# Block-sparse attention with an MLP: the second batch from dense to gathered attention, masks and transposes on TensorE, and a new order of work

## The chip, the cores and the metric

The kernel runs on one core of one Trainium2 chip. A core has five engines, each with its own in-order stream of instructions: TensorE (PE, with its weight loads as PEld), VectorE (DVE), ScalarE (ACT), GpSimd (POOL) and SyncE (SP, which here only issues transfers). They meet through semaphores. The metric is the device time of one execution in microseconds; less is better.

## The reference

Four batches of attention with eight heads, 768 tokens and 64 numbers per head, followed by an MLP over all 3072 tokens (512 to 2048 to 512). Attention is sparse in blocks of 32 tokens, 24 blocks to a side:

```python
scores = (q @ k.T) / sqrt(64)
blk_i, blk_j = pos[:, None] // 32, pos[None, :] // 32
mask = abs(blk_i - blk_j) <= 1
mask = mask | (blk_i == 0) | (blk_j == 0) | (blk_i == 23) | (blk_j == 23)
for qb in range(24):
    for kb in sampled_blocks[qb]:          # three drawn key blocks per query block
        mask[qb*32:(qb+1)*32, kb*32:(kb+1)*32] = True
attn = softmax(where(mask, scores, -1e9))
x = concat over heads of (attn @ v)        # 3072 x 512
out = relu(x @ w_in)**2 @ w_out            # float32
```

The first and the last block of queries see all keys; every other block sees its neighbours, the first and last key block and the three drawn ones.

## The kernel before, in words

A unit `u` is one batch and one pair of heads: 16 units, `HP` = 4 per batch. Matrix work is done in bf16 with 64-row halves of TensorE in pairs (helper `pair`, the line L203 of nearly all matmuls in the profile).

Batches below `SB` (here 2) are **dense**. For a unit, 256 queries and two chunks of 128 keys, `scores` (L343) puts 128 x (2 heads x 2 chunks x 256 queries) into one of four PSUM tiles `X`, ScalarE takes the exponential (`exps`, L360), VectorE multiplies by the 0/1 mask (`masks`, L367) and `values` adds up the product with V, a column of ones giving the sum (`normalize`, L410 and L413). For the first 256 queries of batch 0 the mask is instead added to the scores on TensorE, as a product of two small matrices `oh` and `R2` (argument `add`). The mask tiles for `masks` are kept in the buffers called VG, and are built by `mask_tile` and `mask_evac` from the ranges in `MASKED`.

Batches from `SB` on are **gathered**: for 128 queries, a visit (six per batch), only the keys and values of wanted blocks are brought together. `v_store` writes a batch's V to DRAM; `v_gather` fetches drawn rows with indirect transfers from GpSimd, or with SP's by block numbers in registers; `v_window` fetches the neighbours; `k_gather` (L593 to L599) copies the wanted columns of K into `KG`, on GpSimd or VectorE, with block numbers that `load_blocks` has put in registers (L561). Then `s_scores`, `s_exps` (L623), `s_masks` (L630), `s_values` (L653), `s_normalize` (L659, L662), and `s_transp` turns the 128 x 512 result by a DMA transpose on SP into `xT`.

Queries and keys of batch 0 are transposed on TensorE (`transp`, L305, with `evac`), those of units 4 to 15 by DMA (`transp_dma`). Results of batch 0 are transposed on TensorE (`x_transp`), of batch 1 by DMA (`x_transp_dma`).

The MLP runs in tiles of 256 tokens: `hidden` (product with `w_in`), `relu` (L707 ScalarE, L709 VectorE), `square` (L718 ScalarE, L720 GpSimd), `output` (product with `w_out`), `out_copy` from PSUM to `ys`, and `store`. The last tile's output is split into pieces. Weights come in eight parts, issued by GpSimd (`w_load`, four of w_in and four of w_out); `loads_gate` holds SP's loads for units 4 and on until parts 6 and 7 have come.

The order of everything is one long table, `PROGRAM`: each word has the engine's letter (P, V, A, G, S), the number of a task, and for those that take a PSUM tile its place. `run_program` issues the tasks in this order, so that each engine does its own tasks in the order of its letters, and waits where a task's input isn't ready. The program is written for this one fixed set of buffers.

Of the kernel before, what the change touches and what calls it, by code (L numbers as in the profile page):

```python
# [25 lines left out]
def kernel(  # L26
# [34 lines left out]
    SB, VR, KG_BUFS, VG_BUFS = 2, D + 2, 2, 3  # L61
# [404 lines left out]

    def table_places(e):
# [5 lines left out]
        for i in range(P // block):  # L473
            G.iota(lane[i * block:(i + 1) * block], pattern=[[0, 1]], base=0, channel_multiplier=1, **small)

    def table_slots(e):
        tmp = RT[tb["tmp"][0].at]
        n = SL - 4
        tri, eq = (tmp[0:GR, i * n * SL:(i + 1) * n * SL].rearrange("g (s z) -> g s z", z=SL) for i in range(2))
        al, sm = (tmp[0:GR, 2 * n * SL + i * 2 * SL:2 * n * SL + (i + 1) * 2 * SL].rearrange("g (a s) -> g a s", a=2) for i in range(2))  # L480
        same = tmp[0:GR, 256:256 + 2 * SL * n_rand].rearrange("g (a s r) -> g a s r", a=2, r=n_rand)
        low[0] = RT[tb["tmp"][1].at][0:D].bitcast(BF)[:, 0:5 * P].rearrange("g (s c) -> g s c", c=P)
        V.tensor_copy(out=tab.rearrange("o (g s) -> o g s", s=TS)[:, :, 0:RS],
                      in_=sb_r[:, 2 * n_rand:2 * n_rand * (nb - 1)].rearrange("o (g s two) -> o g s two", g=GR, two=2)[:, :, :, 0])
        V.memset(low[0], 0.0)
        V.tensor_copy(out=ids[:, 6:SL], in_=sb_g.rearrange("g (s two) -> g s two", two=2)[:, :, 0])
        V.tensor_tensor(out=eq, in0=ids[:, 4:SL, None].broadcast_to([GR, n, SL]), in1=ids[:, None, :].broadcast_to([GR, n, SL]), op=AOP.is_equal)
        V.scalar_tensor_tensor(out=eq, in0=before, scalar=0.0, in1=eq, op0=AOP.is_gt, op1=AOP.mult)
        V.tensor_reduce(out=dup, in_=eq, axis=AX.X, op=AOP.max)
        V.tensor_tensor(out=al, in0=ids[:, None, :].broadcast_to([GR, 2, SL]), in1=bl[:, :, None].broadcast_to([GR, 2, SL]), op=AOP.subtract)  # L490
        V.tensor_scalar(out=sm, in0=al, scalar1=-1.0, scalar2=None, op0=AOP.is_ge)
        V.scalar_tensor_tensor(out=al, in0=al, scalar=1.0, in1=sm, op0=AOP.is_le, op1=AOP.mult)
        V.tensor_tensor(out=same, in0=ids[:, None, :, None].broadcast_to([GR, 2, SL, n_rand]),
# [5 lines left out]
        V.tensor_scalar(out=dup, in0=dup, scalar1=-1.0, scalar2=1.0, op0=AOP.mult, op1=AOP.add)  # L499
        V.tensor_tensor(out=al[:, :, 4:SL], in0=al[:, :, 4:SL], in1=dup[:, None, :].broadcast_to([GR, 2, n]), op=AOP.mult)  # L500
        def spread(j, of):
# [8 lines left out]
        V.tensor_scalar(out=half, in0=lane, scalar1=float(HB), scalar2=-float(HB), op0=AOP.is_ge, op1=AOP.mult)  # L510
        V.tensor_tensor(out=lane, in0=lane, in1=half, op=AOP.add)
# [11 lines left out]
    def table_rows(e):  # L523
        V.tensor_scalar(out=idx, in0=low[1][:, P:P + GR], scalar1=float(HB), scalar2=lane, op0=AOP.mult, op1=AOP.add)
        load_blocks("POOL")
        load_blocks("DVE")
        load_blocks("SP")

    def table_masks(g0, g1, e):
        n = g1 - g0  # L530
        for c in range(3):
            copy(e, MKS[:, g0:g1, c].rearrange("p g (e a i) -> p (g e) a i", e=2, a=2) if 0 else MKS[:, g0:g1, c].rearrange("p g (e a i) -> p g e a i", e=2, a=2),
# [36 lines left out]
    def load_blocks(e):  # L569
        for g in wanted[e]:  # L570
# [94 lines left out]
    def s_transp(b, v, e):  # L665
        sy.dma_start(out=x_tile(b, v // 2 * QW)[:, :, v % 2 * P:v % 2 * P + P], in_=xtile.pop(("s", b, v)).rearrange("p a h d -> p (a h d)"), transpose=True)
# [129 lines left out]
    def prepare(u):  # L796
# [4 lines left out]
        if u >= HP:  # L801
# [5 lines left out]
            for w in (1, 0):  # L807
# [4 lines left out]
                x = T_(transp_dma, u, w, deps=[c] + old_s, put=[qc])  # L812
# [131 lines left out]
    for us in [range(b * HP, (b + 1) * HP) for b in range(B)]:  # L944
        for u in us:
            prepare(u)
# [142 lines left out]
```

## Time and profile before

| | us |
|---|---|
| three runs | 261.31, 259.39, 261.24 (median 261.24) |
| profiled execution | 258.88 |
| its span | 257.1 |
| busy: TensorE / ScalarE / VectorE / GpSimd | 243.1 / 183.6 / 171.3 / 98.8 |
| exponentials, dense (72) / gathered, large (48) | 70.6 / 38.0 |
| mask multiplications, dense (60) | 40.9 |
| squares on GpSimd, 1024 wide (11) | 21.6 |

The profile is of one execution; the span is the part of it between the first and the last instruction, and 1.8 us of the execution lie outside. Busy times say how long an engine had an instruction in it. On TensorE, whose instructions overlap in a pipeline, the ends of matmuls are modelled, so its busy time is more than its work at full rate. The line numbers are those of the kernel above; most copies have line L121 or L123 (helper `copy`), and are told apart by their tiles.

### The profile page before, as it was taken

Reading aid. Unit: us, or ns where it says so; the run is one execution under the profiler, and the core shown is the slowest. Engines: PE = TensorE matmul, PEld = TensorE weight load, DVE = VectorE, ACT = ScalarE, POOL = GpSimd, SP = SyncE. Lnnn points to the kernel's source line nnn. Section 1 sums busy time; section 2 is a strip of 40 time slices with the busy share of each in tenths; the row PEclk is TensorE's granted clock in tenths of the full one; section 3 lists DMA queues with packets and bytes.
Section 4 is the critical chain, followed back from the end, with each engine's and each line's share of the span. In section 5 each row is a group of like instructions: output and inputs, shape, how many; then the busy total and the mean of one; then the engine's idle time right before and its main releaser. Section 6 shows DMA issues by size and latency. Waiting matters only on the chain.

```text
span 257.1 us, 12061 instructions
## 1 busy us (share of the span) xinstructions
PE 243.1 (95%) x5265; PEld 182.1 (71%) x5265; DVE 171.3 (67%) x408; ACT 183.6 (71%) x217; POOL 98.8 (38%) x178
## 2 busy tenths in 40 slices
PE   7888999999999997998998999999999999999993
PEld 4667879678874677975864867866875677767683
DVE  7778988899889995969916756657536725730301
ACT  3899999998999797846783975675965286623640
POOL 3183247003316026198556314264357620412100
PEclk9999999999999999999999999999999999999999
DMA  6999989999999996999699779998474923044022
GB/s 200 374 250 207 206 205 155 270 202 252 250 281 179 197 202 153 340 229 154 188 243 202 194 174 167 251 214 199 129 206 95 189 40 60 5 121 148 23 86 83
DMA packets 64692, 47.08 MB, mean 183 GB/s; under 512 B 31567, under 2 KB 60624, under 8 KB 64640
## 3 DMA queue, kind: packets, MB, share of 16 engines
q1 hardware_dynamic: 58512, 37.82, 64.7%
q0 software_dynamic: 5440, 8.05, 16.8%
q8 instruction: 41, 0.67, 1.1%
q10 hardware_dynamic: 688, 0.46, 0.6%
q14 instruction: 11, 0.09, 0.1%
HBM read 35.51 MB, written 7.91 MB: 169 GB/s over the span
## 4 chain that ended last, share of the span: by engine, by line
PE 53%; DVE 5%; DVEq 1%; issue 1%; ACT 1%; ACTq 0%
PE X L203 49%; PE X L653 4%; DVE VB L123 1%; ACT pT L623 1%; DVEq L561 1%; DVE MKS L123 1%; DVE pT L630 1%; DVE r L709 0%; DVE KG L599 0%; DVE qc L123 0%; DVE XS L413 0%; DVE KG L593 0%; DVE XS L662 0%; DVEq L599 0%; DVE rs L410 0%
## 5 line engine op out<-in xcount | busy, mean ns | idle before, releaser
L203 PE MATMUL X<-xT,w_in_sb 64*128 64x256 bf16 x1536 | 100.8, 269 | 2.8 <-issue 1.5
L203 PE MATMUL X<-w_out_sb,g 64*128 64x512 bf16 (+3 forms) x960 | 95.2, 334 | 0.1
L203 PEld LDWEIGHTS <-w_in_sb 64*128 64x128 bf16 x1536 | 74.6, 94 | 16.0 <-issue 5.4
L360 ACT ACTIVATE pT<-X 128x1024 bf16<-128x1024 f32 x72 | 70.6, 1030 | 7.6 <-PE X L203 6.8
L623 ACT ACTIVATE pT<-X 128x768 bf16<-128x768 f32 (+1 forms) x56 | 41.6, 766 | 26.5 <-PE X L203 23.9
L203 PEld LDWEIGHTS <-g 64*128 64x128 bf16 x960 | 40.3, 94 | 26.3 <-PE X L203 0.4
L720 POOL TENSOR_TENSOR g<-r 128x1024 bf16<-128x1024 f32 (+1 forms) x20 | 31.6, 1587 | 64.4 <-ACT r L707 47.2
L707 ACT ACTIVATE r<-X 128x1024 f32<-128x1024 f32 x28 | 29.8, 1068 | 20.6 <-PE X L203 20.5
L709 DVE TENSOR_SCALAR r<-X 128x1024 f32<-128x1024 f32 x20 | 24.5, 1224 | 26.7 <-PE X L203 13.7
L367 DVE TENSOR_TENSOR pT<-pT,VG 128x1024 bf16<-128x1024 bf16 x60 | 40.9, 715 | 0.2
L718 ACT ACTIVATE g<-r 128x1024 bf16<-128x1024 f32 (+1 forms) x40 | 35.2, 899 | 2.7 <-DVE r L709 2.5
L203 PE MATMUL X<-QKT 64*128 64x256 bf16 (+1 forms) x384 | 31.6, 250 | 3.3 <-DVE XS L413 1.3
L630 DVE TENSOR_TENSOR pT<-pT,MKS 128x768 bf16<-128x768 bf16 (+1 forms) x48 | 27.6, 607 | 10.7 <-ACT pT L623 10.5
L203 PEld LDWEIGHTS <-QKT 64*128 64x128 bf16 x384 | 16.7, 95 | 9.5 <-issue 4.1
L579 POOL DMA_INDIRECT VG<-rows,idx x19 | 20.2, 1061 | 4.4 <-issue 2.6
L203 PEld LDWEIGHTS <-pT 64*128 64x128 bf16 x768 | 16.0, 94 | 1.9
L203 PE MATMUL X<-VB,pT 64*128 64x65 bf16 x768 | 17.1, 190 | 0.0
L203 PEld LDWEIGHTS <-KG 64*128 64x128 bf16 x528 | 13.8, 95 | 4.5 <-issue 0.2
L659 DVE RECIPROCAL ss<-X 128x8 f32<-128x8 f32 x12 | 2.5, 206 | 19.5 <-PE X L653 17.3
L653 PEld LDWEIGHTS <-pT 128*64 128x64 bf16 x624 | 11.9, 111 | 4.9 <-issue 3.7
L203 PE MATMUL X<-QKT,KG 64*128 64x64 bf16 x528 | 15.3, 190 | 0.1
L123 POOL CAST VB<-vs 128x768 bf16<-128x768 f32 x9 | 7.8, 869 | 16.5 <-DMA vs<-in_v_dram 16.4
(107 smaller groups left out, 210.3 us busy)
## 6 DMA issues: line engine op xcount, KB each, us to landing
vs<-in_v_dram SPq DMA_DIRECT2D x14, 384.0 KB
ks<-in_k_dram SPq DMA_DIRECT2D x13, 384.0 KB
qs<-in_q_dram SPq DMA_DIRECT2D x12, 384.0 KB
out_dram<-ys SPq DMA_DIRECT2D x9, 512.0 KB
VG<-rows SPq DMA_DIRECT2D x20, 132.0 KB
w_in_sb<-in_moe_w_in_dram POOLq DMA_DIRECT2D x4, 512.0 KB, 8.6
w_out_sb<-in_moe_w_out_dram POOLq DMA_DIRECT2D x4, 512.0 KB, 9.9
rows<-VB SPq DMA_DIRECT2D x2, 792.0 KB
```

Of the source, the lines that this page charges most:

```text
L123: (V if e == "DVE" else G).tensor_copy(out=out, in_=in_)
L203: last = nc.tensor.matmul(out(r ^ crossed), lhsT(r ^ crossed, rows), rhs(r ^ crossed, rows), skip_group_check=True, **kw)
L360: A.activation(out=pT[:, :, 0:n], in_=stile.pop(a)[:, :, 0:n], func=AF.Exp, scale=scale)
L367: V.tensor_tensor(out=pT, in0=pT, in1=m[:, None].broadcast_to([P, 2, len(cs), w]), op=AOP.mult)
L579: G.indirect_dma_start(out=to[0:RS * HB], out_offset=None, in_=pairs, in_offset=bass.IndirectOffsetOnAxis(ap=idx[0:RS * HB, g - 1:g], axis=0))
L623: A.activation(out=pT[:, :, 0:n], in_=stile.pop((u, v, gs))[:, :, 0:n], func=AF.Exp, scale=scale)
L630: V.tensor_tensor(out=pT, in0=pT, in1=m[:, None].broadcast_to([P, 2, n]), op=AOP.mult)
L653: nc.tensor.matmul(po[i * D:(i + 1) * D, h, a * VW:(a + 1) * VW], pts[g][:, h, c * D:(c + 1) * D], val, start=a == 0 and c == 0, stop=c == ...
L707: A.activation(out=to, in_=src, func=AF.Relu)
L709: V.tensor_scalar(out=to, in0=src, scalar1=0.0, scalar2=None, op0=AOP.max)
L718: A.activation(out=g, in_=r, func=AF.Square)
L720: (G if e == "POOL" else V).tensor_mul(out=g, in0=r, in1=r)
```

## The change

`SB` becomes 1: batch 1, too, is done by gathering, so there are 18 visits instead of 12, and the table of drawn blocks is needed earlier. `MASKED` becomes empty: all masks of batch 0 are added on TensorE, and mask tiles and mask multiplications no longer exist. `BY_PE` names units 4 to 7, whose queries and keys are transposed on TensorE instead of by DMA. `s_transp` becomes eight TensorE transposes into spare columns of the visit's own PSUM tile, followed by a copy out (`s_evac`) on VectorE or ScalarE, which then frees the tile. The table's work is cut into five smaller tasks that use `ys` buffers instead of `r` buffers, and `load_blocks` into two parts per engine. The order of all tasks is new. A word with letter S for a transpose still means that the instruction is issued on TensorE at that place.

```diff
-    SB, VR, KG_BUFS, VG_BUFS = 2, D + 2, 2, 3
+    SB, VR, KG_BUFS, VG_BUFS = 1, D + 2, 2, 3
...
     GATES = (6, 7)
+    BY_PE = range(HP, 2 * HP)
-    MASKED = ((256, 512), (512, 768), (0, 256))
+    MASKED = ()
...
+    def table_scratch():
+        tmp = [YS[b_.at] for b_ in tb["tmp"]]
...
-    def table_slots(e):
-        tmp = RT[tb["tmp"][0].at]
...
+        low[0] = table_scratch()[-1]
+        G.memset(low[0], 0.0)
+
+    def table_ids(e):
...
+    def table_dup(e):
...
+    def table_near(e):
...
+    def table_drawn(e):
...
+    def table_low(e):
...
     def table_rows(e):
         V.tensor_scalar(out=idx, in0=low[1][:, P:P + GR], scalar1=float(HB), scalar2=lane, op0=AOP.mult, op1=AOP.add)
-        load_blocks("POOL")
-        load_blocks("DVE")
-        load_blocks("SP")
...
-    def load_blocks(e):
-        for g in wanted[e]:
+    def load_blocks(g0, g1, e):
+        for g in [g_ for g_ in wanted[e] if g0 <= g_ < g1]:
             if g not in held_at[e]:
                 held_at[e][g] = blocks_of(g, ENGINE[e])
...
-    def s_transp(b, v, e):
-        sy.dma_start(out=x_tile(b, v // 2 * QW)[:, :, v % 2 * P:v % 2 * P + P], in_=xtile.pop(("s", b, v)).rearrange("p a h d -> p (a h d)"), transpose=True)
+    def s_transp(b, v, buf, e):
+        xs = xtile.pop(("s", b, v))
+        pt = tile_of(buf)[:, :, 384:512].bitcast(BF).rearrange("p r (a i) -> p r a i", i=D)
+        for a in range(HP):
+            for r, rows in enumerate(HALVES):
+                nc.tensor.transpose(pt[:, r, a], xs[rows, a].rearrange("p h d -> p (h d)"), identb[rows, rows])
+        xtile["t", b, v] = pt
+
+    def s_evac(b, v, e):
+        to = x_tile(b, v // 2 * QW)[:, :, v % 2 * P:v % 2 * P + P]
+        copy(e, to.rearrange("q a (r i) -> q r a i", r=2), xtile.pop(("t", b, v)))
...
-                x = T_(transp_dma, u, w, deps=[c] + old_s, put=[qc])
+                if u in BY_PE:
+                    hb = Buf("X")
+                    t = T_(transp, u, w, ALL, hb, deps=[c], get=[hb], put=[qc])
+                    x = T_(evac, u, w, ALL, deps=[t] + old_s, put=[hb])
+                else:
+                    x = T_(transp_dma, u, w, deps=[c] + old_s, put=[qc])
...
-        nm = T_(s_normalize, b, v, deps=[va], get=[xs], put=[yb, ot])
-        mu["s", b, v] = T_(s_transp, b, v, deps=[nm] + x_get(b, v // 2 * QW), put=[xs])
+        nm = T_(s_normalize, b, v, deps=[va], get=[xs])
+        xt = T_(s_transp, b, v, yb, deps=[nm], put=[xs])
+        mu["s", b, v] = T_(s_evac, b, v, deps=[xt] + x_get(b, v // 2 * QW), put=[yb, ot])
...
-    tmp = tb["tmp"] = [Buf("r"), Buf("r")]
-    tb["slots"] = T_(table_slots, deps=[t, p], get=tmp)
+    tmp = tb["tmp"] = [Buf("ys"), Buf("ys")]
+    p = T_(table_places, get=tmp)
+    i_ = tb["ids"] = T_(table_ids, deps=[t, p])
+    for e_ in ("POOL", "DVE", "SP"):
+        T_(load_blocks, 0, 4, deps=[i_])
+        T_(load_blocks, 4, nb, deps=[i_])
...
-            attend(a, us[0] < HP and a[1] == 0)
+            attend(a, True)
...
-        A29 G35 P4/3 V32 P30/0 P12/2 P14/3 P9/1 P5/1 V31 P33/1 V111 P36/3 P0/2 A37 V1 V34 P102/2 V209 V46 P47/0 P106/1 A103 V48 P104/3
...
+        A36 P4/0 P37/1 P12/2 P14/3 G42 P9/0 P5/2 V39 V38 P40/3 P43/0 P0/2 V100 A44 V1 V41 P91/1 V53 V183 A92 P54/2 P95/0 V55 P93/3 V50
...
```

Three places of the new order follow. The first is GpSimd's stream at the start. Before, behind the copy that waits for the third load of V, stand the weight loads (`w_in_sb`, `w_out_sb`; a row with x2 is two parts), casts of V (`VB`) and of queries (`qc`), and squares (`g` from `r`):

```order
L328 DMA w_in_sb<-in_moe_w_in_dram 128x4x512 x2
L123 CAST VB_189<-vs_80 128x2x6x64
L123 CAST qc_107<-qs_74 128x512
L328 DMA w_in_sb<-in_moe_w_in_dram 128x4x512
L123 CAST VB_189<-ys_85 128x2x6x64
L123 CAST qc_109<-qs_75 128x512
L328 DMA w_in_sb<-in_moe_w_in_dram 128x4x512
L331 DMA w_out_sb<-in_moe_w_out_dram 128x4x512 x2
L720 TENSOR_TENSOR g_94<-r_81 128x512
L331 DMA w_out_sb<-in_moe_w_out_dram 128x4x512
```

Now the table's places (`MKS`, `ids`, `bl`, `lane`, `ys`) and one cast are ahead of two parts of w_out and the last of w_in:

```order
L485 MEMSET ys_86 64x640
L124 CAST qc_107<-KG_119 128x512
L332 DMA w_out_sb<-in_moe_w_out_dram 128x4x512 x2
L575 TENSOR_LOAD tab
L329 DMA w_in_sb<-in_moe_w_in_dram 128x4x512
L743 TENSOR_TENSOR g_95<-r_82 128x512 x2
```

and the other two parts of w_out come a dozen instructions later:

```order
L124 CAST qc_107<-ks_79 128x384 x2
L743 TENSOR_TENSOR g_98<-r_82 128x1024
L124 CAST VB_192<-vs_80 128x2x6x64
L332 DMA w_out_sb<-in_moe_w_out_dram 128x4x512 x2
L743 TENSOR_TENSOR g_99<-r_83 128x512 x2
```

So two parts of w_out (6 and 7, those that the gate waits for) moved ahead of the last part of w_in, and the other two behind squares and a cast of the second batch's V.

The second place is TensorE at the end of a visit. Before, as here behind the last visit in its order, a visit's value matmuls (`VG`, `pT`) were followed by hidden work:

```order
L653 MATMUL X_149<-VG_209,pT_90 64x65
L203 LDWEIGHTS w_in_sb
L203 MATMUL X_147<-xT_117,w_in_sb 128x256
L203 LDWEIGHTS w_in_sb
L203 MATMUL X_147<-xT_117,w_in_sb 128x256
```

Now, at the third visit of batch 3 for one, the transposes of the normalized result (`XS`) stand directly behind the last value matmul, eight pairs of rows of which the first and the last are shown here:

```order
L667 LDWEIGHTS pT_87
L667 MATMUL X_149<-VG_210,pT_87 64x65
L684 LDWEIGHTS XS
L684 MATMUL X_149<-identb,XS 128x64
...
L684 LDWEIGHTS XS
L684 MATMUL X_149<-identb,XS 128x64
L204 LDWEIGHTS KG_119
L204 MATMUL X_148<-QKT,KG_119 128x64
```

What moved is a step that was on SP's queue; it now stands in TensorE's stream between that visit's values and the scores of the next.

The third place is the end of SP's stream: stores of the output (`ys` and `qs` hold pieces of it). Before:

```order
L779 DMA out_dram<-ys_85 64x512
L781 DMA out_dram<-ys_85 128x512
L776 DMA out_dram<-ys_84 128x2x512
L776 DMA out_dram<-ys_85 128x512
L776 DMA out_dram<-qs_74 128x256
L776 DMA out_dram<-qs_76 128x128
```

Now:

```order
L802 DMA out_dram<-ys_86 64x512
L804 DMA out_dram<-ys_86 128x512
L799 DMA out_dram<-qs_77 128x128
L799 DMA out_dram<-ys_85 128x2x512
L799 DMA out_dram<-ys_86 128x512
L799 DMA out_dram<-qs_75 128x256
```

The store of the smallest piece, `qs` 128x128, moved from last to fourth from last; the three larger ones are behind it.

More of the change, by code (lines that the diff above doesn't have):

```diff
@@ L509, in table_slots @@
         spread(4, ids)
-        V.tensor_scalar(out=half, in0=lane, scalar1=float(HB), scalar2=-float(HB), op0=AOP.is_ge, op1=AOP.mult)
-        V.tensor_tensor(out=lane, in0=lane, in1=half, op=AOP.add)
     def table_spread(buf, e):
@@ L891, in visit @@
         cl = T_(v_claim, b, v, get=[vb], deps=mk_claims[-1:])
-        parts = [T_(v_gather, b, v, i, deps=[vw, cl, tb["rows"], tb["slots"]]) for i, g in enumerate(VISITS[v]) if g]
+        parts = [T_(v_gather, b, v, i, deps=[vw, cl, tb["rows"], tb["ids"]]) for i, g in enumerate(VISITS[v]) if g]
         for t_, g in zip(parts, gs_):
@@ L897, in visit @@
         for g in [g for g in VISITS[v] if g]:
-            kc[g] = T_(k_gather, b, v, g, get=[] if kc else [kb], deps=[ev[u][1, 0] for u in us] + [tb["slots"]] + list(kc.values()))
+            kc[g] = T_(k_gather, b, v, g, get=[] if kc else [kb], deps=[ev[u][1, 0] for u in us] + [tb["ids"]] + list(kc.values()) + (sum((cq[u, w] for u in (2, 3) for w in (0, 1)), []) if b == SB else []))
             kc[g].blocks = g, ("POOL", "DVE")
```

136 lines of the change are left out of this document (72 added, 64 removed).

## The prediction

> **What bounds the kernel now.** I began with the page's busy times and its row of transfer rates, and then read the span in stretches of 20 us (start:end and length, then busy us and, in brackets, instructions of PE, PEld, DVE, ACT and POOL, then clock, DMA share, GB/s).
>
> ```profile
> PE 243.1 (95%) x5265; PEld 182.1 (71%) x5265; DVE 171.3 (67%) x408; ACT 183.6 (71%) x217; POOL 98.8 (38%) x178
> GB/s 200 374 250 207 206 205 155 270 202 252 250 281 179 197 202 153 340 229 154 188 243 202 194 174 167 251 214 199 129 206 95 189 40 60 5 121 148 23 86 83
> ```
>
> ```profile
> 20.00:40.00 20.00, 18.89 (x394) 15.57 (x392) 17.82 (x38) 19.39 (x24) 7.49 (x9) 1.00 1.07 194
> 40.00:60.00 20.00, 19.73 (x447) 15.70 (x445) 17.43 (x35) 19.65 (x23) 3.21 (x11) 1.00 1.17 232
> 100.00:120.00 20.00, 18.20 (x425) 14.74 (x426) 16.56 (x44) 12.30 (x17) 12.24 (x17) 1.00 1.03 225
> 180.00:200.00 20.00, 20.00 (x460) 14.01 (x453) 10.41 (x22) 14.22 (x18) 11.54 (x20) 1.00 0.58 145
> ```
>
> TensorE bounds the whole, but not everywhere alone: until 60 us ScalarE is 97 to 98% busy and VectorE 87 to 89%, so there three engines are near their end; from 180 us on only TensorE is. The clock column is 1.00 throughout, so no term below is one of clock.
>
> A busy TensorE still need not run at its rate, since ends are modelled. The waits that the profile names for it (engine, line, what it waited for: total, times, longest) come to little; these three lead:
>
> ```profile
> PE X L203 <- issue: 1.7, 5, 0.4
> PE X L203 <- DVE XS L413: 1.3, 2, 1.0
> PE X L203 <- DVE bm L192: 1.2, 1, 1.2
> ```
>
> So I priced each of the 5265 matmuls by the distance at which its form follows itself where nothing is late (rows further down) and set the running sum against the clock. It is 227.7 us, and the last matmul ends at 253.3. The clock is ahead of the sum by 4.2 us when the first masks are added (6.4 us), 12.4 at 32.6, 15.6 at 95.6, 23.1 at 148 and 25.6 at the end. These differences are my estimate; at its ends stand these rows (start, duration, then the group), the last of them the final store on SP:
>
> ```profile
> 6.40 0.27 PE L203 MATMUL X<-R,oh 64*128 64x256 bf16 x2
> 6.51 0.27 PE L203 MATMUL X<-QKT 64*128 64x256 bf16 x2
> ...
> 252.66 0.63 PE L203 MATMUL X<-w_out_sb,g 64*128 64x64 bf16 x32
> 253.50 0.33 SPq L776 DMA_DIRECT2D out_dram<-qs  x1
> ```
>
> TensorE's time is thus 227.7 of work, 4.2 before it, **21.4 lost in between** (8.2 until 32.6, 3.2 until 95.6, 7.5 until 148, 2.5 in the last 105), and 3.8 from the last matmul to 257.1. The change has to be judged on the work, on the 21.4 and on the 3.8.
>
> **TensorE's work.** The distances, from rows at which the next group starts without a wait (next start minus own start):
>
> ```profile
> 61.20 0.40 PE L203 MATMUL X<-QKT 64*128 64x256 bf16 x4
> 61.42 1.05 PE L203 MATMUL X<-xT,w_in_sb 64*128 64x256 bf16 x16
> 62.29 0.54 PE L203 MATMUL X<-VB,pT 64*128 64x65 bf16 x24
> 62.66 0.61 PE L203 MATMUL X<-xT,w_in_sb 64*128 64x256 bf16 x8
> ...
> 161.31 0.35 PE L203 MATMUL X<-QKT,KG 64*128 64x64 bf16 x12
> 161.48 0.83 PE L203 MATMUL X<-w_out_sb,g 64*128 64x512 bf16 x6
> ...
> 165.08 0.95 PE L653 MATMUL X<-VG,pT 128*64 128x65 bf16 x48
> 165.96 1.05 PE L203 MATMUL X<-xT,w_in_sb 64*128 64x256 bf16 x16
> 166.84 0.34 PE L203 MATMUL X<-QKT 64*128 64x64 bf16 x12
> 167.02 1.04 PE L203 MATMUL X<-xT,w_in_sb 64*128 64x256 bf16 x16
> ...
> 12.85 0.34 PE L305 MATMUL X<-identb,qc 64*128 64x64 bf16 x12
> 13.04 0.28 PE L203 MATMUL X<-QKT 64*128 64x256 bf16 x2
> ```
>
> Four dense score matmuls take .22, 24 dense value matmuls .37, twelve KG scores .17, twelve scores against the first block .18, a visit's 48 values .88, a mask pair .11, twelve transposes .19. The dense second batch goes: 36 slots less of .22 (−7.9) and 24 groups less of .37 (−8.9). Its gathered form comes: 22 x .17 (+3.7), 4 x .18 (+.7), five visits' values at .88 and the first visit, half as long again, taken at 1.7 (+6.1). The masks of batch 0 on TensorE add 39 pairs (+4.3); transposing batch 1's queries and keys adds 96 matmuls (+1.5); transposing each visit's result adds 18 x 8, at the same .016 each (+2.3). Sum: **+1.8 us**. The gathered batch saves only 6.3, and masks and transposes give 8.1 back.
>
> The Trainium skill's page "TensorE: Matmul & The Clock Gate", section "Wait — 56ns, not 53.3ns?", says that matmuls never start closer than about 25 ns, however small. The row of twelve in .17 us is 14 ns each, so here a pair on the two row halves must count as one start (28 ns); taken per matmul, the rule would make these terms dearer, and my estimate of the sum would then be +3.6 instead of +1.8.
>
> **The other engines.** By shape (line, engine, form, count, then busy us, mean ns):
>
> ```profile
> L360 ACT ACTIVATE pT<-X 128x1024 bf16<-128x1024 f32 x72 | 70.6, 1030 | 7.6 <-PE X L203 6.8
> L367 DVE TENSOR_TENSOR pT<-pT,VG 128x1024 bf16<-128x1024 bf16 x60 | 40.9, 715 | 0.2
> L623 ACT ACTIVATE pT<-X 128x768 bf16<-128x768 f32 x48 | 38.0, 811 | 21.8 <-PE X L203 19.7 <-PE X L653 1.9
> L630 DVE TENSOR_TENSOR pT<-pT,MKS 128x768 bf16<-128x768 bf16 x40 | 23.3, 613 | 10.7 <-ACT pT L623 10.5
> L720 POOL TENSOR_TENSOR g<-r 128x1024 bf16<-128x1024 f32 x11 | 21.6, 1968 | 36.0 <-ACT r L707 24.2 <-DVE r L709 11.7
> L579 POOL DMA_INDIRECT VG<-rows,idx x19 | 20.2, 1061 | 4.4 <-issue 2.6 <-PE X L203 0.9 <-DVE pT L630 0.3
> L599 POOL COPY KG<-QKT 128x64 int32 x60 | 11.8, 242 | 0.0
> L599 DVE COPY KG<-QKT 128x64 int32 x72 | 9.7, 205 | 0.0
> L659 DVE RECIPROCAL ss<-X 128x8 f32<-128x8 f32 x12 | 2.5, 206 | 19.5 <-PE X L653 17.3 <-PE X L203 2.0
> L662 DVE TENSOR_TENSOR XS<-X,ss 128x512 bf16<-128x512 f32 x12 | 8.3, 692 | 0.4
> ```
>
> ScalarE loses 36 exponentials (70.6/72 = .98 each) and gains 24 of .79 and four half-sized: about −16 to −20 us, nearly all within the first third, where it is full. VectorE loses all 60 mask multiplications (−40.9) and gains 20 s_masks of .58 (+11.6), a visit's normalize six more times, 13 evacuations of transposed results and copies of keys, and stays near its old sum. GpSimd takes what is left: squares go from 11 to 20 of 1.97 and from nine to seven of the half size (+15.5), indirect gathers from 19 to 27 (+8.5), block copies from 68 to 102 of .24 and the other gather pieces (+11), casts and the table (+5): **98.8 to about 139 us**. In its own order the heavy stretches fall at the first visits of batch 1, where I count 15 to 16.6 us of GpSimd in 15.5 us of TensorE's work, and VectorE 17.3 to 18.7 with it. In the stretches above GpSimd stood at 12.24 of 20 when the first gathers ran.
>
> **The 21.4 lost us.** Until 32.6 us the exponentials set the pace: by TensorE's work position 30 ScalarE was given 38.8 us of work before and 32.8 in the change, so I let 2.0 of the 8.2 go (between 0, if the loads and first casts stand behind it, and 5, if all of ScalarE's relief counts). The loads of w_out parts 4 and 5 are now issued behind a cast of V and a square on GpSimd, about 46 us by its order, and the first output wants part 4 at about 54. A load of this size took 9.9 us to land (the row below, its last number the median), so by these places it would be 2 us late; if it lands as fast as the rate of 374 GB/s lets 512 KB, it isn't, and behind a busier GpSimd it is 3. I take +2.0:
>
> ```profile
> w_out_sb<-in_moe_w_out_dram POOLq DMA_DIRECT2D x4, 512.0 KB, 9.9
> ```
>
> Between 32.6 and 148 us 10.7 are lost. The worst single place, where VectorE's mask casts and block-number loads (the chain of waits, start, duration) stood ahead of a normalize, is taken apart by the change: the table work is cut into small pieces and moved early.
>
> ```profile
> 99.20 0.86 DVEq L561
> ...
> 100.43 0.43 DVE XS L413
> ...
> 100.91 12.49 PE X L203 x318
> ```
>
> From there on I use the rate of the last 105 us, 2.5, for the 150 us that come after the gathering begins (+3.8), and 1.5 for the first gathered stretch, in which GpSimd and VectorE are full. What is new is that transposes wait on TensorE, in order, for VectorE's reciprocal and multiplication (206 and 692 ns by the rows above, with the semaphores between them 1.05 us); hidden and output matmuls are queued behind them. In the order, two of the 18 stand directly behind their s_values and one .6 us of TensorE's work behind, the others 1.7 to 4 us: 1.05 + 1.05 + .45 = 2.5 us. In all 6.2 + 2.0 + 1.5 + 3.8 + 2.5 = 16.0, against 21.4: **−5.4** (from −11, with the early loads in time and visits as smooth as the last 105 us, to +1, if nothing of 8.2 and 10.7 goes and the new waits come).
>
> The 26 DMA transposes that go, and the stores and loads of one more batch of V rows, are moves of the queues; none of the three waits above names a transfer, so I price them at nothing (between −1 and +1 us).
>
> **The end.** SP now stores, behind the 64 KB piece that waits for the last copy, a piece of 512 KB, one of 256 and one of 128. Before, one 64 KB piece was left there, and 3.8 us passed from the last matmul. Three more issues at .33 are +1.0; .96 MB at the best rate of the page's slices, 374 GB/s, are 2.6 us against next to nothing. Bounds 0 (if the last copy is done earlier) and +3.1; the transfers decide, so I take **+2.4**.
>
> **Sum.** +1.8 −5.4 +2.4 = −1.2 us: 258.88 for the profiled run becomes 257.7; the median shown, 261.24, is 2.4 above that run, so 260.0 us by it. No change that a measurement of this kernel could tell from none (about 1%).
>
> **Rivals.**
> *The early third decides (faster).* ScalarE's relief counts in full and nothing new is late: 21.4 falls by 10 rather than 5.4. For it: 97% in the stretches to 60 us; against it: VectorE is nearly as full there. −1.2 −4.6 = −5.8: 255.4, and with the tail hidden 253.
>
> *GpSimd decides (slower).* Its copies of keys stand in order behind squares of 1.97 us, TensorE's s_scores wait for them and the hidden work ahead runs out. It decides once GpSimd's work in a stretch passes TensorE's, which by my count it does in one to two stretches of 15 us, by up to 1.1 us, plus the register loads that are not counted as busy; a square ahead of a late gather costs 1.97 each. Two or three of these: +4 to +6: 264 to 266. Against it: before, GpSimd's longest idle time was behind relus, not the reverse. The Trainium skill's page "SBUF — State Buffer", section "🔬 SBUF: two separate sides", says that GpSimd and VectorE share a port pair which one holds for a whole instruction while the other blocks. By that rule each of the nine further large squares could hold VectorE up for as long as it lasts; the rows above, with copies of 242 and 205 ns in the mean, show no such hold of a square's length.
>
> *The lost time stays (same to slower).* It was startup and loads, not ScalarE: no −5.4, hence +4.2: 265.4; with half of it, 262.7.
>
> *The order does not bind.* That gathered rows and transposes cost nothing since TensorE was idle anyway: excluded by the 20.00 of 20 in the last stretch, where all of it is TensorE's own time.
>
> **How the numbers follow.** The forecast with its neighbours within 1% (258.6 to 263.8) .36; the early third .35; GpSimd .18; the lost time stays .11, with its half inside the forecast. The range takes in the faster rival to 253.5 and GpSimd to 267. Faster by over 1%: .35, within: .36, slower: .29.
>
> **What would show it.** In the changed profile: ScalarE well under 90% between 20 and 60 us with TensorE near 20 of 20 (step of 2.0); waits of TensorE on transposes for VectorE's L676 multiplication, three of about 1 us; a wait for w_out near 54 us; GpSimd near 139 us, not ahead of TensorE in its waits; and from the last matmul to the end about 6 us. I am wrong if TensorE waits for keys (KG) by several us, if the chain runs over GpSimd, or if TensorE's waits before 60 us are as they were.

## The result, and the profile after

| | median us | ratio to the kernel before | 95% interval |
|---|---|---|---|
| kernel before | 260.41 | 1 | |
| changed kernel | 284.62 | 1.092 | 1.084 to 1.100 |

The change makes the kernel 9% slower, 24 us; the range ended at 267. Here and below a time is the median of all runs, while a ratio compares fast runs alone, without executions that lie over 1.5% above the fastest of their kernel, so it can differ from the quotient of the medians by some tenths of a per cent. The profiled execution took 285.5 us, its span 283.7. The busy row of its page and four stretches of 20 us (columns as before):

```profile
PE 251.3 (89%) x5487; PEld 181.9 (64%) x5487; DVE 175.6 (62%) x412; ACT 154.1 (54%) x193; POOL 150.7 (53%) x260
```

```profile
20.00:40.00 20.00, 19.43 (x394) 15.59 (x390) 10.01 (x33) 16.34 (x19) 8.90 (x21) 0.94 1.13 213
40.00:60.00 20.00, 17.24 (x472) 14.56 (x474) 14.09 (x36) 13.81 (x17) 10.21 (x14) 1.00 0.89 216
60.00:80.00 20.00, 17.28 (x339) 11.86 (x340) 13.32 (x35) 8.85 (x15) 17.32 (x31) 1.00 0.78 219
180.00:200.00 20.00, 18.64 (x378) 12.73 (x374) 9.95 (x21) 10.25 (x13) 12.20 (x18) 1.00 0.92 175
```

ScalarE is relieved as forecast (16.34 of 20 where it had 19.39), but TensorE isn't busier for it: from 40 us on it stands at 17 to 19 of 20 in every stretch, where before it reached 20. The named waits of TensorE are longer and more, and still only a part ("issue" is time for which the profile shows nothing that was waited for):

```profile
PE X L204 <- issue: 5.1, 6, 1.2
PE X L684 <- DVE XS L676: 3.1, 3, 1.1
PE X L399 <- POOL VB L124: 3.0, 1, 3.0
PE X L204 <- DVE KG L613: 2.1, 2, 1.2
```

Priced with one table of distances, the work itself rose by 1.3 us, from 227.7 to 229.0. The last output matmul ends at 277.0 us, so the clock is then 48.0 us ahead of the sum, 4.1 of them before the first masks are added: 43.9 us lost in between, where the kernel before lost 21.4 and I had forecast 16.0. About 34 of the 43.9 lie behind 32.6 us. Like the sums of the prediction, these are estimates.

By shape (line, engine, form, count, busy us, mean ns), the rows that answer to those of before:

```profile
L361 ACT ACTIVATE pT<-X 128x1024 bf16<-128x1024 f32 x36 | 34.6, 1027 | 8.4 <-PE X L204 6.7 <-PE X L399 1.6
L644 DVE TENSOR_TENSOR pT<-pT,MKS 128x768 bf16<-128x768 bf16 x60 | 44.4, 774 | 8.3 <-ACT pT L637 8.3
L743 POOL TENSOR_TENSOR g<-r 128x1024 bf16<-128x1024 f32 x20 | 39.6, 1982 | 26.8 <-DVE r L732 19.3 <-ACT r L730 7.5
L732 DVE TENSOR_SCALAR r<-X 128x1024 f32<-128x1024 f32 x25 | 30.3, 1223 | 29.3 <-PE X L204 28.7 <-POOL KG L613 0.5
L613 POOL COPY KG<-QKT 128x64 int32 x90 | 20.9, 278 | 0.0
L607 DVE COPY KG<-QKT 128x256 int32<-128x256 int32 x18 | 12.5, 694 | 0.0
```

The mask multiplication of a visit takes 774 ns where it took 613, VectorE's first copy of keys 694 where it took 349. The relu of VectorE, which reads PSUM and writes SBUF, is unchanged (1224 and 1223). So something makes instructions of VectorE longer that read and write SBUF, though not all: its casts of queries and keys (128x384) stay at 541 to 545 ns. What it is can be seen at 220 us, in the rows of VectorE and then of GpSimd (start, duration):

```profile
221.80 5.61 DVE L644 TENSOR_TENSOR pT<-pT,MKS 128x768 bf16<-128x768 bf16 x5
227.33 1.21 DVE L732 TENSOR_SCALAR r<-X 128x1024 f32<-128x1024 f32 x1
...
222.77 1.91 POOL L743 TENSOR_TENSOR g<-r 128x1024 bf16<-128x1024 f32 x1
224.61 0.41 POOL L607 COPY KG<-QKT 128x256 int32<-128x256 int32 x1
224.95 1.10 POOL L613 COPY KG<-QKT 128x64 int32 x6
```

Five multiplications take 5.61 us; four of them about .55, and one 3.7: it begins with GpSimd's square at 222.8 and ends .4 us after the last of the seven copies that follow it. Over the trace, 14 large multiplications with no GpSimd instruction beside them take .54 to .56 us, 46 with one take .84 in the mean.

### The profile page after: what moved, and what is told of

Its sections match the earlier page's. It is cut to its first block, busy times and chain, and to the rows that moved or that the text cites. A ratio compares the mean times of both kernels' runs of the same rounds, so it can differ in the third digit from the quotient of the medians.

```text
span 283.7 us, 12688 instructions
## 1 busy us (share of the span) xinstructions
PE 251.3 (89%) x5487; PEld 181.9 (64%) x5487; DVE 175.6 (62%) x412; ACT 154.1 (54%) x193; POOL 150.7 (53%) x260
## 4 chain that ended last, share of the span: by engine, by line
PE 65%; DVE 10%; DMA 8%; issue 5%; SPq 5%; POOL 3%; ACT 2%; DVEq 0%; POOLq 0%; ACTq 0%
PE X L204 56%; PE X L667 5%; DMA ys<-in_v_dram 3%; DVE pT L644 3%; PE X L399 2%; DMA VG<-rows,idx 2%; DMA QKT<-qc 2%; SPq L170 2%; SPq L596 1%; PE X L684 1%; POOL qc L124 1%; DVE r L732 1%; DVE XS L676 1%; DVE KG L613 1%; SPq L802 1%
## 5 line engine op out<-in xcount | busy, mean ns | idle before, releaser
L637 ACT ACTIVATE pT<-X 128x768 bf16<-128x768 f32 (+1 forms) x84 | 62.7, 764 | 58.9 <-PE X L204 51.8
L743 POOL TENSOR_TENSOR g<-r 128x1024 bf16<-128x1024 f32 (+1 forms) x33 | 52.9, 1611 | 67.0 <-DVE r L732 50.2
L644 DVE TENSOR_TENSOR pT<-pT,MKS 128x768 bf16<-128x768 bf16 (+1 forms) x72 | 50.5, 733 | 13.3 <-ACT pT L637 10.1
L732 DVE TENSOR_SCALAR r<-X 128x1024 f32<-128x1024 f32 x25 | 30.3, 1223 | 29.3 <-PE X L204 28.7
L361 ACT ACTIVATE pT<-X 128x1024 bf16<-128x1024 f32 x36 | 34.6, 1027 | 8.4 <-PE X L204 6.7
L741 ACT ACTIVATE g<-r 128x1024 bf16<-128x1024 f32 (+1 forms) x27 | 23.3, 879 | 16.0 <-DVE r L732 15.8
L730 ACT ACTIVATE r<-X 128x1024 f32<-128x1024 f32 x23 | 25.0, 1085 | 12.6 <-PE X L204 11.1
L204 PE MATMUL X<-QKT,KG 64*128 64x64 bf16 x792 | 23.7, 190 | 6.6 <-issue 2.2
L204 PE MATMUL X<-QKT 64*128 64x256 bf16 (+1 forms) x288 | 22.7, 235 | 2.1 <-ACT pT L637 0.8
L667 PEld LDWEIGHTS <-pT 128*64 128x64 bf16 x936 | 17.9, 111 | 6.5 <-issue 4.8
L667 PE MATMUL X<-VG,pT 128*64 128x65 bf16 x792 | 19.7, 197 | 1.3 <-issue 0.7
L613 POOL COPY KG<-QKT 128x64 int32 x90 | 20.9, 278 | 0.0
L204 PE MATMUL X<-R,oh 64*128 64x256 bf16 x144 | 18.5, 279 | 0.0
```

The lines of the kernel that those rows point to most:

```text
L204: last = nc.tensor.matmul(out(r ^ crossed), lhsT(r ^ crossed, rows), rhs(r ^ crossed, rows), skip_group_check=True, **kw)
L361: A.activation(out=pT[:, :, 0:n], in_=stile.pop(a)[:, :, 0:n], func=AF.Exp, scale=scale)
L613: eng.tensor_copy(out=rows[:, :, :, r_ * w:(r_ + 1) * w], in_=src[:, :, :, bass.ds(at[r_] * w, w)])
L637: A.activation(out=pT[:, :, 0:n], in_=stile.pop((u, v, gs))[:, :, 0:n], func=AF.Exp, scale=scale)
L644: V.tensor_tensor(out=pT, in0=pT, in1=m[:, None].broadcast_to([P, 2, n]), op=AOP.mult)
L667: nc.tensor.matmul(po[i * D:(i + 1) * D, h, a * VW:(a + 1) * VW], pts[g][:, h, c * D:(c + 1) * D], val, start=a == 0 and c == 0, stop=c == ...
```

## Experiments

Each ratio is to runs of the kernel before on the same chip, which has its median at 256 to 262 us.

### Waits between halves: taken out of the changed kernel, put into the kernel before

Half of the array's rows accumulate a group's first half, then the other half of the rows writes into the same bank; `change_places` makes the second half wait for the first. In the order before, one of the 48 hidden groups has its second half directly behind the first, in the changed order 24. There the trace shows 24 hidden matmuls in 1.55 us (next start minus own start) where at the rate of 16 in .87 they would take 1.31:

```profile
98.82 1.71 PE L204 MATMUL X<-xT,w_in_sb 64*128 64x256 bf16 x24
100.37 0.31 PE L204 MATMUL X<-QKT,KG 64*128 64x64 bf16 x10
```

I had not looked for this in the order. Two runs, one for each direction (two places shown of each):

```diff
-  P749 A174 P750 P751 P177/2 S89 P762/1          (changed kernel)
+  P749 A174 P762/1 P750 P751 P177/2 S89
-  P771 P235/1 G803
+  P235/1 P771 G803
```

> The changed kernel with its work as it is, and only TensorE's order altered: at the 28 places where the second half of a hidden, output or value group stands directly behind its first half (each half on the other rows of the array, into the bank that the first has just written), one other piece of TensorE's work is put between the two. Theory 'halves': the trace of the changed kernel shows 29 waits of hidden matmuls on TensorE's own matmuls, .28 us each, 8.0 us, against five before; they go, and the time falls by 6 to 8 us, to about 277.5. Rival 'the waits stand beside others': what is gained here is lost at the next wait for VectorE or GpSimd, and the time falls by less than 2.

```diff
-  P782 V178 P189/3 P783 V51                      (kernel before)
+  P782 P783 V178 P189/3 V51
-  P775 A144 V191 G78 P186/3 P181 P776
+  P775 P776 A144 V191 G78 P186/3 P181
```

> The kernel before, with the reverse: 26 second halves (24 of hidden, two of values) are moved directly behind their first halves, nothing else. Theory 'halves': 26 x .28 = 7.3 us more, about 268 us where the kernel before has 260.5. Rival 'the waits stand beside others': under 2 us more.

Measured: 284.16 us, ratio 1.088 [1.080, 1.097] for the changed kernel with halves apart: nothing that the measurement can tell. 266.75 us, 1.0225 [1.014, 1.031] for the kernel before with 26 halves together: 5.8 us, .22 for each. So the wait is real and costs where TensorE is the bound, and in the changed kernel it costs nothing that can be measured: 6.6 us of such waits are gone from its trace, but TensorE waits for VectorE and ScalarE instead.

```profile
PE X L684 <- DVE XS L676: 3.1, 3, 1.1
PE X L667 <- DVE pT L644: 2.7, 4, 1.4
PE X L204 <- DVE KG L613: 2.6, 2, 1.6
PE X L428 <- DVE xq L414: 2.4, 2, 2.2
PE X L204 <- ACT r L730: 2.3, 3, 1.8
```

These are the waits of TensorE with the halves apart; the values' wait for masks (L667 for L644) was .3 in the changed kernel, and that for a relu (L730) is new.

### The start: V ahead of the weights

`G59` is the cast of the second unit's V, `G82` and `G83` are weight loads.

```diff
-  V73 G82 A113 P75/3 P114/1 V76 G83 V70 P99 A115 P122/3 V101 G59
+  V73 G59 G82 A113 P75/3 P114/1 V76 G83 V70 P99 A115 P122/3 V101
```

> The changed kernel with one word moved: on GpSimd the cast of the second unit's V stands ahead of the first weight loads (which wait for the third V to land) rather than behind two of them. Theory 'the start': the 3.0 us that TensorE waits for this cast at 15.3 to 18.4 us go, and the time falls by 2.5 to 3.5 us, to about 281.5. Rival 'ScalarE or the clock sets the start': the time stays within 1 us, since the next exponentials are late instead.

Measured: 280.82 us, ratio 1.078 [1.066, 1.090], some 3.5 us less; the interval overlaps that of the changed kernel, so it is the traces that show the gain. In the changed kernel GpSimd takes V's cast behind two loads that wait for the third V to land, and TensorE waits 3.04 us for it:

```profile
18.38 1.06 PE L399 MATMUL X<-VB,pT 128*128 128x65 bf16 x24 [3.04 <-POOL VB L124]
```

With the word moved the cast runs at 12.44 us and the same values at 15.30. Behind the wait the granted clock of the changed kernel is .51, from 18.9 to 22.3 us, and in the repaired one it is 1.00 there. TensorE was busy for 3.2 us of that stretch, so by my estimate up to 1.6 us of the gain are clock. By the running sum the repaired kernel is then 13.4 us behind at 32 us of work, the kernel before 13.1: ScalarE's relief bought nothing there.

### The end: stores in the order of their data

```diff
-  P1194 P1195 A1166 P17/3 P16/1 S1187 P13/3 A1196 P11/1 S1197 S1129 S1167 V1176 S1177
+  P1175 V1176 S1177 P1165 A1166 S1167 ... P1194 P1195 P17/3 P16/1 S1187 P13/3 A1196 P11/1 S1197
```

`S1129`, the 512 KB store, went up behind its copy `V1128`.

> The changed kernel with the last stores in the order in which their data comes: the 512 KB store right behind its copy, then the 128 KB and 256 KB ones, and the two 64 KB ones last; two copies of the last tile moved up to stand right behind their matmuls. Theory 'the end': from the last matmul to the end 3.8 us as before instead of 6.5, so 2.5 us less, about 282. Rival 'the transfers bind': the same bytes have to go out after the same matmuls, and under 1 us is gained.

Measured: 281.25 us, ratio 1.0745 [1.065, 1.084], about 4 us less, more than forecast. In this trace, too, the granted clock is 1.00 from 10 to 40 us, so by the estimate above up to 1.6 of the 4 us need not be the end's. SP's last rows in the changed kernel, where the first of them waits for the copy ahead of it:

```profile
277.26 0.27 ACT L122 COPY qs<-X 128x128 f32<-128x128 f32 x1 [0.57 <-PE X L204]
277.55 0.36 SPq L799 DMA_DIRECT2D out_dram<-qs  x1
278.01 1.50 SPq L799 DMA_DIRECT2D out_dram<-ys  x2
279.60 0.78 SPq L799 DMA_DIRECT2D out_dram<-qs  x1
```

From the start of the last output matmul to the end it is 7.0 us here, 4.0 in the kernel before, 3.7 with the stores in order.

### GpSimd's squares: to ScalarE in the changed kernel, to GpSimd in the kernel before

```diff
-  P235/1 G803 S240        (changed kernel, 20 such words)
+  P235/1 A803 S240
```

> The changed kernel with the 20 large squares of GpSimd done by ScalarE at the same places of the order (ScalarE is 54% busy, GpSimd 53%); nothing else. Theory 'GpSimd holds VectorE up': in the changed kernel a large mask multiplication of a visit takes 774 ns in the mean where it took 613, and a first copy of keys on VectorE 694 where it took 349; with the squares gone from GpSimd they go back to about 620 to 660 and 350 to 450, some 12 us of VectorE, and the time falls by 5 to 9 us, to about 277. Rival 'the order is tight whoever does it': ScalarE's 20 squares of 1.05 us stand ahead of exponentials, and the time stays within 2 us.

```diff
-  V936 A897 P492/1        (kernel before, 9 such words)
+  V936 G897 P492/1
```

> The kernel before, with the reverse: nine large squares of ScalarE, the first nine after the first gathered scores, are done by GpSimd, so that it has 20 as in the changed kernel. Theory 'GpSimd holds VectorE up': the large mask multiplications rise from 613 to about 680 ns, and the time by 2 to 5 us. Rival 'no engine but TensorE binds there': within 1 us.

Measured: 274.23 us, ratio 1.064 [1.053, 1.074], with the squares on ScalarE: about 7 us of the 24. And 268.78 us, ratio 1.049 [1.042, 1.056], for the kernel before with nine squares more on GpSimd: 12.5 us, 1.4 for each, more than forecast. VectorE's busy time says how. In the changed kernel with the squares on ScalarE, without any change to its own work it falls from 175.6 to 157.3 us,

```profile
PE 249.6 (92%) x5487; PEld 181.3 (67%) x5487; DVE 157.3 (58%) x412; ACT 171.8 (63%) x213; POOL 110.2 (41%) x240
```

the mask multiplications to 611 ns and the first copies of keys to 365. In the kernel before with nine squares more they rise to 878 ns:

```profile
L630 DVE TENSOR_TENSOR pT<-pT,MKS 128x768 bf16<-128x768 bf16 x40 | 33.7, 878 | 7.3 <-ACT pT L623 7.2
```

and one place shows the mechanism at its worst, a pair of multiplications that takes 7.58 us, one of them 7.11, as long as GpSimd has instruction upon instruction (VectorE's row, then GpSimd's):

```profile
147.57 7.58 DVE L630 TENSOR_TENSOR pT<-pT,MKS 128x768 bf16<-128x768 bf16 x2
155.08 0.20 DVE L659 RECIPROCAL ss<-X 128x8 f32<-128x8 f32 x1
...
147.28 3.75 POOL L720 TENSOR_TENSOR g<-r 128x1024 bf16<-128x1024 f32 x2
150.97 0.40 POOL L593 COPY KG<-QKT 128x256 int32<-128x256 int32 x1
151.31 1.10 POOL L599 COPY KG<-QKT 128x64 int32 x6
152.38 1.88 POOL L720 TENSOR_TENSOR g<-r 128x1024 bf16<-128x1024 f32 x1
```

Behind it TensorE waits 5.5 us, at values of a visit, for the normalize (`XS`) that VectorE does next. Another wait of this kind, 2.9 us, stands 28 us earlier, and these two are the longest waits of TensorE in this run:

```profile
PE X L653 <- DVE XS L662: 5.5, 1, 5.5
PE X L203 <- DVE XS L662: 2.9, 1, 2.9
```

No wait of .2 us or more is for a square or a copy of GpSimd, so it isn't late squares that TensorE waited for. The Trainium skill's page "SBUF — State Buffer", section "🔬 SBUF: two separate sides", gives the rule: VectorE with two SBUF inputs, or in one of its modes that use two ports, and GpSimd reading SBUF take one port pair in turn, for a whole instruction. The trace agrees that multiplications with two SBUF inputs are held up, and goes further: the hold lasted over ten of GpSimd's instructions. The copies of keys, which have one input, are longer too; in which mode they ran no run here shows.

Not all of the 12.5 us are waits. With and behind the two waits the granted clock was at half:

```profile
128.80:132.20 3.40, 3.40 (x64) 3.04 (x60) 3.08 (x10) 2.75 (x4) 2.49 (x8) 0.50 1.08 339
152.70:159.50 6.80, 3.45 (x68) 2.31 (x69) 6.73 (x18) 0.81 (x1) 2.66 (x2) 0.50 0.29 70
```

TensorE was busy for 6.85 us there, an estimated 3.4 us of loss, and the mean clock of all four runs of this kernel was .979 to .986, where the runs of the kernel before beside them had .999 to 1.000. So 1.4 us for each square is a mean, made up of a few long holds and the clock behind them, and not the price of a square.

### Half-sized squares

```diff
-            (G if e == "POOL" else V).tensor_mul(out=g, in0=r, in1=r)
+            m = 2 * w if e == "POOL" else n * w
+            for z in range(0, n * w, m):
+                (G if e == "POOL" else V).tensor_mul(out=g[:, z:z + m], in0=r[:, z:z + m], in1=r[:, z:z + m])
```

> The changed kernel with each of the 20 large squares of GpSimd issued as two of half the size, one behind the other; nothing else. In the changed kernel a mask multiplication of .55 us took up to 3.7 us, and 7.1 in the run with nine squares added to the kernel before, as long as GpSimd ran instruction upon instruction. Theory 'VectorE gets its turn when GpSimd's instruction ends': it now waits half as long, the large mask multiplications fall from 774 to about 660 to 700 ns, and the time by 2 to 5 us. Theory 'VectorE gets no turn as long as GpSimd's next instruction is there': they stay at 760 or more, and the time stays or rises by up to 3 us, since two halves take 2.1 to 2.2 us where one took 1.98.

Measured: 280.72 us, ratio 1.090 [1.080, 1.100]: no time gained. The large multiplications fall to 709 ns, the longest from 3.7 to 1.6 us, so VectorE does get turns between halves. But its first copies of keys rise from 694 to 764 ns, the longest from 2.3 to 3.2 us, and its busy time as a whole falls by 1.3 us only. Neither theory holds whole: the hold does end at some of GpSimd's boundaries, and at others, as with the copies above, it doesn't. Which ones stays open.

### Repairs together

The first kernel has the halves, the start and the end as above, and the transposes of four visits moved down, for example

```diff
-  P721/3 V722 S723 P1087 P1088 V725        (P721 values, V722 normalize, S723 transposes)
+  P721/3 V722 P1087 P1088 S723 V725
```

The second kernel of the two has the 20 large squares on ScalarE as well.

> The changed kernel with all repairs of its order at once: second halves apart (28 places), the cast of V ahead of the weight loads, the last stores in the order of their data, and the transposes of four visits moved behind at least 1.35 us of TensorE's work after their values. Theory 'waits of TensorE add up': halves 6.6, start 3, end 3, transposes 3.6 less: about 268.5. Theory 'another engine sets the pace between': what was gained at the halves alone did not show in the time, so only start and end (6) and a part of the rest: 274 to 277.

> The two runs beside this together: all repairs of the order, and the 20 large squares on ScalarE. Theory 'GpSimd holds VectorE up, and that hid the gain of the halves': the gains add up and more, 262 to 267. Rival 'tight order': as with the repairs alone, within 2 us.

Measured: 276.71 us, ratio 1.080 [1.072, 1.088], without the squares; 269.53 us, 1.050 [1.044, 1.057], with them. The first says that waits don't add up: 16 us of them were to go, and some 3 us are gained (0 to 6 by the two intervals). The squares are worth the same 3% with the repairs as without; the forecast that the gains add up and more, 262 to 267, was missed, since a ratio of 1.050 is 273 us where the kernel before takes 260.4.

The kernel with halves apart and squares on ScalarE, and nothing else (both edits as above), asks whether VectorE's lateness is what hid the gain of the halves:

> The changed kernel with two repairs alone: second halves apart (28 places, which alone gave nothing that can be measured), and the 20 large squares of GpSimd on ScalarE (which alone brought the ratio to the kernel before from 1.092 to 1.064). Start, end and transposes stay. Theory 'the halves gave nothing because VectorE, held up by GpSimd, set the pace': their 6.6 us of waits now count, and the ratio comes to 1.035 to 1.05. Rival 'such waits stand beside others in this order whoever holds whom': the ratio stays at 1.055 to 1.07.

Measured: 274.04 us, ratio 1.065 [1.058, 1.071], as with the squares alone. My theory fell, the rival stands: in this order a wait of TensorE between halves is time that it would spend at the next wait, also with the large squares gone from GpSimd. In its trace the halves' waits are some 7 us less than with the squares alone, and those behind normalizes, exponentials, relus and the pauses told of below are more.

All 33 squares on ScalarE, the small ones too, with all repairs:

> The changed kernel with all repairs of its order and all 33 squares of GpSimd on ScalarE, the 13 half-sized ones too. Theory 'GpSimd beside VectorE is what is left': large mask multiplications from 611 to about 580 ns, ratio to the kernel before from 1.050 to 1.03 to 1.045. Rival 'what is left lies in the stretch of the table and first gathers, and in run-out instructions': the ratio stays between 1.04 and 1.06, since ScalarE's 8 us more are late for exponentials there.

Measured: 269.04 us, ratio 1.044 [1.038, 1.051], not to be told from 1.050. The large multiplications fall to 599 ns. The small squares are at most a small part of what is left.

The reverse in the kernel before, to see whether its own squares cost it something:

```diff
-  V435 P482/3 G903 P904/2      (9 such words)
+  V435 P482/3 A903 P904/2
```

> The kernel before with the nine large squares that GpSimd does after the first gathered scores done by ScalarE at the same places; nothing else. Its large mask multiplications are at 613 ns, .55 alone. Theory 'what GpSimd holds up counts here too': they fall to about 570, and the time by 1 to 3 us, faster than both kernels. Rival 'the order of before keeps them apart already': within 1 us, or up to 2 us slower where ScalarE's squares stand ahead of exponentials.

Measured: 258.78 us, ratio 1.0047 [1.001, 1.008]. No gain: in its trace, of an execution of 261.22 us, the multiplications stay at 617 ns, the longest at 1.9 us. No version beats the kernel before.

### Pauses without a releaser

The largest item of TensorE's waits is "issue", 5.1 us. These pauses stand in the middle of a group of like matmuls, where no semaphore is waited for. Counted over the records of TensorE, they come at the same counts in kernels with different work there: after matmul 1119 in eleven of the traces (1118 in the kernel before), after 2139, 2521, 2776, 3031 in many, all at 172 to 192 of a count by 256 instructions (a matmul and its weight load are two), and those of .45 us and more end, but for a few, 2.2 to 2.9 us after a 16 KB transfer of instructions has begun; there are 43 such transfers for the stream's 11,000 instructions, 256 in each. Two runs were made on it, the first with

```diff
+    for _ in range(64):
+        nc.tensor.nop()
```

> The changed kernel with 64 empty instructions on TensorE ahead of everything, which shift all later ones by 64 places. In seven traces TensorE's pauses of .5 to 1.4 us for which nothing releases it stand 2.2 to 2.9 us behind the start of a 16 KB instruction transfer, and at the same place, 174 to 190, of a count by 256 instructions. Theory 'it has run out of instructions': the pauses come 64 instructions earlier in the work (32 matmuls), at other groups; those at matmuls 1119, 2139, 2521 and 3031 go, others come, their sum stays between 3 and 6 us. Rival 'a wait that the trace does not name': they stay at the same matmuls.

It took 279.79 us in one run, and says nothing: the instruction count of its trace is that of the changed kernel, the empty instructions were not in it. The second:

```diff
-    N_WARM, N_IDLE = 14, 14
+    N_WARM, N_IDLE = 6, 14
```

> The changed kernel with six instead of fourteen pairs of warming matmuls ahead of the first work, 32 instructions of TensorE less, where it waits anyway; all else stays. (The 64 empty instructions of an earlier run do not appear in its trace, which has as many instructions as the changed kernel's, so that run said nothing on this.) Theory 'TensorE has run out of instructions': the pauses without releaser stay at the same counts of the stream, that is at matmuls near 1119, 2139, 2521 and 3031 counted from the start, though other work, 16 matmuls later, stands there. Rival 'a wait of that work that the trace does not name': they move with the work, to 1103, 2123, 2505 and 3015.

Measured: 277.45 us in one run. The pauses are after 1119, 2139 and 3031, as in the changed kernel, with work there that is 16 matmuls further on. The pause after 2139 in the changed kernel, and then in this one:

```profile
111.77 0.26 PE L204 MATMUL X<-QKT,KG 64*128 64x64 bf16 x6 [0.80 <-issue]
```

```profile
107.87 0.32 PE L204 MATMUL X<-QKT,KG 64*128 64x64 bf16 x10 [1.35 <-issue]
```

So the pauses belong to the stream of instructions and not to the work, and the rival falls. That TensorE has run out of instructions is the reading that fits: 128 matmuls on hidden work last 7 us; the same count of KG matmuls, at 12 in .17 us by the rows of before, lasts 1.8, less than the 2.2 to 2.9 that pass from the start of such a transfer to the end of a pause. The "issue" rows of the profile come to 6.2 us in the changed kernel, 3.9 of them at these counts; to 2.3 us in the kernel before, .6 of them at these counts; and to 1.7 to 5.7 us in the other edits of the changed kernel. That the gathered batch costs this is argued from these counts, and not shown; no run took the pauses away alone.

## Why the prediction was wrong, point by point

- **TensorE's work, +1.8.** Right: +1.3 with one table of distances.
- **The end, +2.4.** Right: +3.0 by the trace from the last output matmul on, and putting the stores in order gave most of it back.
- **Transposes behind their values, 2.5.** Nearly right: three waits, 3.1 us idle, at the places that the order shows.
- **ScalarE's relief, −2.0 until 32.6 us.** Wrong. ScalarE fell from 19.39 to 16.34 of 20, and with the start repaired TensorE was as far behind as before. ScalarE's busy share had been no bound that TensorE waited for.
- **The start.** Missed: a cast on GpSimd stands behind weight loads which wait for a transfer, 3.0 us. I had named the weight loads' order, not what they stand in front of on GpSimd.
- **w_out parts 4 and 5, +2.0.** Did not happen; TensorE waits for no weights.
- **"From there on I use the rate of the last 105 us, 2.5 ... and 1.5 for the first gathered stretch".** This is the step that failed. It put 5.3 us on the lost time of everything behind 32.6 us, 9.8 with the waits for transposes and weights; by the running sum about 34 were lost there. (A rate of 2.5 us in 105 gives 3.6 for 150 us, not the 3.8 that I wrote, which changes nothing.) It assumed that VectorE and GpSimd beside each other keep the durations that they had. GpSimd went to 150.7 us, 12 more than forecast, and VectorE came "near its old sum", 175.6, but some 18 of VectorE's are time in which large squares on GpSimd hold it up: without them its sum is 157.3. That moving large squares between GpSimd and ScalarE is worth 7 us in the changed kernel and 12.5 in the kernel before is shown by two runs in opposite directions, some 3.4 of the 12.5 through the clock by my estimate. So this accounts for 7 of the 24 us; the forecast for the whole, 16.0 lost, came out at 43.9.
- **The rival "GpSimd decides"** had the right engine and the wrong place: not late copies of keys by GpSimd, but masks and copies of VectorE held up. Its price, 4 to 6 us, was near the 7 that the squares are worth. I set the port rule aside because the mean copies showed "no such hold of a square's length". A mean of 60 copies can't show it; the row to read was the mask multiplication's spread. In the kernel before, 16 large ones alone take .555 us, 24 beside GpSimd .652, and one of them 2.25.
- **The halves.** Not seen. They cost 5.8 us where TensorE is the bound and nothing that can be measured here.
- **What is left.** With all repairs and all squares moved the kernel is still 4.4% slower, 11 us. Pauses without a releaser (4.8 us of "issue" in that trace, 2.3 before) and 1.3 us of work are a part; the stretch from 32 to 56 us of work, in which the table and the first gathers lie, costs 4.9 us there and 1.6 before, one pause of 1.6 included. The rest isn't settled.

## What to carry to other kernels

Before work is moved to GpSimd, look at what VectorE does at the same time: if it multiplies two SBUF tensors there, a GpSimd instruction can be paid on both engines, and the price is seen in the longest instruction of a group, not in its mean. Waits of TensorE can't be added up in a tightly ordered kernel: 6.6 us of them were free in one order, and 7.3 cost 5.8 in the other, and only a run that removes or adds them tells which. And count instructions as well as time: by these traces long runs of small matmuls can outrun the instruction stream.

## What the runs showed of the hardware that was not expected

- VectorE was held up for 7.1 us by GpSimd, over two squares, seven copies and a third square, for a multiplication that takes .55 alone; with squares of half the size the longest such multiplication took 1.6 us, and a copy of keys 3.2.
- TensorE pauses for .3 to 1.6 us with nothing to wait for, in most cases at fixed counts of its stream, 2.2 to 2.9 us behind the start of a transfer of 256 instructions.
- A second half of rows that writes the bank of the first waits .28 us if nothing stands between.
- The granted clock stood at half in the middle of some traces, each time with or behind a wait of TensorE: for 3.4 us from 18.9 us in the changed kernel, behind 3.0 us for V; for 3.4 us from 18.5 us in the one with all repairs and the large squares moved, behind 1.6 us for a normalize; for 3.4 and 6.8 us in the kernel before with nine squares more. Behind a wait of 2.4 us for V, in the run with the stores in order, it stayed at 1.00, so the length of the wait alone doesn't say when it falls, and what sets it is open.
